# A quarter of a weight conversion moved to GpSimd, an earlier first score, and matmuls padded to one tiling

## The chip, the cores and the metric

The kernel runs on one core of a Trainium2 chip. The metric is the device time of that core in microseconds (us), the median of several executions. A core has five engines that each work through their own list of instructions in order and meet only at semaphores: TensorE (PE, its weight loads shown as PEld), VectorE (DVE), ScalarE (ACT), GpSimd (POOL) and SyncE (SP), which here only issues transfers.

## The reference, cut to what matters

There are 8 batches, 8 heads, 576 tokens and a head size of 64. For each head, attention keeps only the 32 largest scores of a row; the heads are put side by side to a row of 512 channels, and an FNet block with a two-layer channel network follows.

```python
scores = scale * np.matmul(q, k.transpose(0, 1, 3, 2))
kth = np.partition(scores, -32, axis=-1)[..., -32:-31]
scores = np.where(scores >= kth, scores, -1e9)
attn = softmax(scores)                     # exp(scores - max) / (sum + 1e-9)
x = heads_side_by_side(attn @ v)           # (8, 576, 512)
u = x + np.real(fft(fft(x, axis=1), axis=2))
un = (u - mean(u)) / np.sqrt(var(u) + 1e-6)
out = u + np.maximum(un @ w_ch1, 0.0) @ w_ch2   # 512 -> 2048 -> 512
```

The arrays q, k and v are float32; the two weight matrices come as float64[...], so they are converted in the kernel.

## The kernel before, in words

**Items and steps.** Two heads form a pair, so a batch has 4 pairs and the whole input 32. The 576 queries of a head are cut into four blocks of 128 and a tail block of 64 (two times 32 rows, one from each half of the sequence). The tail blocks of both heads of a pair share one tile. A pair therefore has 9 items (`IN_PAIR`), a batch 36 (`PER_BATCH`) and the whole input 288. One main loop over `i` makes one step for each item, and each step puts, by hand, some work on every engine: the scores of item `i + 3` (`scores`), the top-32 search of item `i` and the first half of that of `i + 1` (`top_ops`), the mask (`mask`), the exponential (`expo`), the transposes of the probabilities (`transposes`), and now and then the product with v (`attend`). Work that is due at a given step is stored by `at(step, where, fn)` and is put out when the loop reaches that step and place.

**The top-32 search** is on VectorE: per item four `max` (L350) and three `match_replace` (L352) over 576 scores. Two values per row then go to GpSimd, which forms the bounds `nt` (L359); ScalarE makes from them a penalty (`Relu`, L366); GpSimd subtracts it from the scores (L367); ScalarE takes the exponential (L373); TensorE transposes the result (L394, L405). So each item goes VectorE, GpSimd, ScalarE, GpSimd, ScalarE, TensorE, and GpSimd stands in this chain twice.

**The weight conversion** is in the first batch only. There are 32 chunks of 128x512 numbers, one started in nearly every step (`start_of`). A chunk n with start s0 is loaded as pairs of 32-bit words into one of five slots (`space`). At step s0 + 1 ScalarE scales the high words into a PSUM tile (`scale_high`, L169) and makes two other words ready (`rest`, L185 and L188); VectorE shifts the scaled word left by 3 bits into the weight tile (`shift`, L176); GpSimd adds the low bits and multiplies by the sign (`join`, L195 and L196). When the join is done, the slot is free and chunk n + 5 is loaded. For columns of the first layer, GpSimd also subtracts a mean later (`centre`, L912): eight such instructions fall in the first batch.

**The Fourier part of a batch** begins when its attention is done. VectorE or GpSimd folds the channels (`fold_ops`, `fold_tails`), TensorE multiplies by tables (`dft_tokens`, L594), once for even and once for odd frequencies, so two passes per batch and 16 in all. In a pass, the stationary operand has 128 rows for the two full token blocks (`fg`, `zw`) and 64 for the tail tokens (`ft`). After `dft_channels` the two-layer network (`hidden` L737 and `back` L761) is cut into units that are put between the attention work of the next batch, as a rule of the loop decides (`level`, `some`).

**Tail scores.** The keys of the tail tokens are multiplied in a matmul of their own (`scores` with `part == 1`, L299), with a block-diagonal key tile `kt` of 128x128. For the 128-row items, the stationary operand is 128 queries; for the tail item it is 64. The trace writes the shape of the array that an instruction uses as rows times columns of the stationary operand, such as 128\*64.

**The start.** All of q of pair 0 is loaded and transposed before k; k goes through a tile of its own. The tail scores of item 0 use the same two PSUM tiles as the full scores and are copied by ScalarE.

Of the kernel before, what the change touches and what calls it, by code (L numbers as in the profile page):

```python
# [18 lines left out]
P = 128  # L19
# [45 lines left out]
def kernel(  # L65
# [57 lines left out]
    nat_t = const.tile([P, NC, 2, D], F32, name="nat", tag="nat")  # L123

    kt_t = const.tile([P, P], F32, name="kt", tag="kt")
    v_t = [const.tile([P, NC, 2, D], F32, name=f"v{i}", tag=f"v{i}") for i in range(2)]


# [19 lines left out]
    def weight_steps(chunks, space, wc, slots):  # L148

        scaled = {}  # L150

        def words(n):
            o = 2 * wc * (n % slots)
            raw = space[:, o:o + 2 * wc]
            return raw, raw[:, 0:2 * wc:2], raw[:, 1:2 * wc:2]

        def load(n):
            if n < len(chunks):
                dst, src = chunks[n]
                if moe_w_ch1.dtype == F32:  # L160
                    nc.sync.dma_start(out=dst, in_=src)
                else:
                    nc.sync.dma_start(out=words(n)[0].bitcast(I32), in_=src.bitcast(I32))

        def scale_high(n):
            if moe_w_ch1.dtype == F32:
                return
            scaled[n] = ps_m.tile([P, wc], F32, name=f"wh_{n}", tag="mm")
            nc.scalar.activation(  # L169
                out=scaled[n], in_=words(n)[2], func=AF.Copy, scale=2.0 ** -112  # L170
            )

        def shift(n):
            if moe_w_ch1.dtype == F32:
                return
            nc.vector.tensor_scalar(  # L176
                out=chunks[n][0].bitcast(I32), in0=scaled.pop(n).bitcast(I32),
                scalar1=3, scalar2=None, op0=ALU.logical_shift_left,
            )

        def rest(n):
            if moe_w_ch1.dtype == F32:
                return
            _, low, high = words(n)
            nc.scalar.activation(  # L185
                out=low.bitcast(I32), in_=low.bitcast(U32), func=AF.Copy, scale=2.0 ** -29
            )
            nc.scalar.activation(out=high, in_=high.bitcast(I32), func=AF.Sign)  # L188

        def join(n):  # L190
            if moe_w_ch1.dtype == F32:
                return
            dst, (_, low, high) = chunks[n][0], words(n)
            bits = dst.bitcast(I32)
            nc.gpsimd.tensor_tensor(out=bits, in0=bits, in1=low.bitcast(I32), op=ALU.add)  # L195
            nc.gpsimd.tensor_tensor(out=dst, in0=dst, in1=high, op=ALU.mult)  # L196

        return load, scale_high, shift, rest, join


    nat, qT_of, kT_of, v_of, PT, Ssb, Wk, Wp, M8, Nt = ({} for _ in range(10))
# [3 lines left out]

    def load_full(dst, src, pair, queue=None):
        b, hp = divmod(pair, NPB)
        for e in range(2):  # L210
            s2 = src[b, 2 * hp + e].rearrange("(h r) d -> h r d", h=2)
            for h in range(2):
                (queue or nc.sync).dma_start(
                    out=dst[:, 2 * h:2 * h + 2, e, :],
                    in_=s2[h, 0:2 * P, :].rearrange("(t p) d -> p t d", p=P),
                )

    def load_tails(dst, src, pair, row0=(0, 0)):
        b, hp = divmod(pair, NPB)
        for e in range(2):  # L220
            s2 = src[b, 2 * hp + e].rearrange("(h r) d -> h r d", h=2)
            for h in range(2):
                r0 = row0[e] + TH * h
                nc.sync.dma_start(out=dst[r0:r0 + TH, NF, e, :], in_=s2[h, 2 * P:HS, :])

    def load_nat(n, pair, dst=None, queue=None):
        if pair < NPAIR:
            nat[n, pair] = nat_t if dst is None else dst
            src = q if n == "q" else k
            load_full(nat[n, pair], src, pair, queue)  # L230
            load_tails(nat[n, pair], src, pair)

    def load_v(pair):
# [2 lines left out]
            load_full(v_of[pair], v, pair)  # L236
            load_tails(v_of[pair], v, pair, (0, TAIL))

    def prep(n, pair):

        if pair >= NPAIR:
            return 0.0
        src = nat.pop((n, pair))
        t_sb = attp.tile([P, S if n == "q" else NF * P], F32, name=f"{n}T_{pair}", tag=f"{n}T")
        for c0, c1 in ((0, NF), (NF, NC)):
            tp = ps_t.tile([P, 4, P], F32, name=f"tp{n}_{pair}_{c0}", tag="tp")
            for c in range(c0, c1):
                nc.tensor.transpose(  # L248
                    tp[:, c - c0, :], src[:, c, :, :].rearrange("p h d -> p (h d)"), ident
                )  # L250
            if c0 == 0:
                dst, got = t_sb[:, 0:NF * P], tp.rearrange("p a c -> p (a c)")
            else:
                dst, got = t_sb[:, NF * P:], tp[:, 0, 0:TAIL]
            if n == "q":
                nc.scalar.mul(out=dst, in_=got, mul=scale)
            elif c0 == 0:
                nc.scalar.copy(out=dst, in_=got)
            else:
                for hd in (slice(0, D), slice(D, P)):  # L260
                    nc.scalar.copy(out=kt_t[hd, hd], in_=got[hd])
        (qT_of if n == "q" else kT_of)[pair] = t_sb
        return 0.7


# [8 lines left out]
    def scores(i, part):  # L274
# [20 lines left out]
                (Ssb[i + 1], slice(0, P), slice(TAIL, S), slice(0, TAIL)),  # L295
            ]
        if part == 1:
            sp = ps_s.tile([P, NF * P], F32, name=f"sp_{i}_t", tag="sp")
            nc.tensor.matmul(  # L299
                sp[0:rows, 0:P], lhsT=qT[:, q_cols], rhs=kt_t, start=True, stop=True  # L300
            )
            for h, (s_t, r, _, tails) in enumerate(to):
                nc.scalar.copy(out=s_t[r, tails], in_=sp[0:rows, TAIL * h:TAIL * (h + 1)])  # L303
            return 0.3
        if e is None and i >= PER_BATCH:

# [201 lines left out]
        return ap.rearrange("p (m two) -> p two m", two=2)  # L508

    Q1, Q2, Q3 = DM // 4, DM // 2, 3 * DM // 4  # L510
    ROWS3 = (P, P, TAIL)
    folded, ft_of, y_of, yt_of, us_of, rs_of, unT_of = ({} for _ in range(7))

    def fold_channels(eng, z, f, n):

# [18 lines left out]

    def fold_tails(b, eng):


        z = batp.tile([P, DM], F32, name=f"zt_{b}", tag="fold_s")[0:TAIL]
        ft_of[b] = batp.tile([P, DM + 1], F32, name=f"ft_{b}", tag="fold_t")
        f = ft_of[b][0:TAIL]  # L540
        fold_halves(eng, x_of[b][0:TAIL, 4, :], z)
        for n in range(2):
            fold_channels(eng, z, f[:, 0:DM], n)
        eng.tensor_copy(out=f[:, DM:DM + 1], in_=z[:, Q1:Q1 + 1])
# [34 lines left out]
    def dft_tokens(b, par):  # L579
# [1 line left out]
        while any(u[2] == "hidden" for u in queue):  # L581
            one_unit()
        _, zw, fg = folded[b, par]
        tails = ft_of[b]
        if b not in y_of:
            y_of[b] = batp.tile([P, 4, S], F32, name=f"y_{b}", tag="y")
        y = y_of[b]
# [4 lines left out]
        def mm(g2, gg, st, lhsT, rows, table, start=False):  # L592

            nc.tensor.matmul(  # L594
                yps[g2][0:rows, gg, :],
                lhsT=lhsT[0:ROWS3[st]],
                rhs=fs[0:ROWS3[st], table, par, st, :],
                start=start,
                stop=st == 2,
                skip_group_check=True,  # L600
            )

        for g2 in range(2):
            for gg in range(2):
                g = 2 * g2 + gg
                for st in range(2):
                    mm(
                        g2, gg, st, fg[:, st, P * g:P * (g + 1)], P, gg,  # L610
                        start=gg == 0 and st == 0,
                    )
        for st in range(2):
            mm(0, 1, st, zw[:, st, Q1:Q1 + 1], 1, 0)
        mm(0, 1, 2, tails[:, DM:DM + 1], 1, 0)
        for g2 in range(2):
            for gg in range(2):
                g = 2 * g2 + gg
                mm(g2, gg, 2, tails[:, P * g:P * (g + 1)], P, gg)

        mir, back = (
            (slice(HS + 2, S, 2), slice(KQ - 2, 0, -1)) if par == 0
# [218 lines left out]
    nc.vector.memset(cc[:, 0:1], -1.0)  # L841

    warm = small.tile([P, 1], F32, name="warm", tag="rd", bufs=6)
    nc.scalar.activation(out=warm, in_=cc[:, 0:1], func=AF.Exp)
    nc.vector.memset(cc[:, 1:2], FAR)
    for t in mv + den_t:
        nc.vector.memset(t, 1.0)

    kn0 = batp.tile([P, NC, 2, D], F32, name="kn0", tag="y")
    for t in v_t:  # L850
        nc.gpsimd.memset(t[TAIL:P, NF, 0, :], 0.0)
        nc.gpsimd.memset(t[0:TAIL, NF, 1, :], 0.0)
    for t in (nat_t, kn0):
        nc.gpsimd.memset(t[TAIL:P, NF, :, :], 0.0)
    nc.gpsimd.memset(kt_t, 0.0)

    nc.scalar.dma_start(out=ident, in_=id_d.ap())
    load_nat("q", 0)
    load_nat("k", 0, kn0, nc.scalar)
    prep("q", 0)  # L860
    prep("k", 0)


# [10 lines left out]
    wcs = weight_chunks(w1, moe_w_ch1, NDT, WC) + weight_chunks(w2, moe_w_ch2, NIT, WC)  # L874
    n1 = NDT * DF // WC
    AHEAD = 5
    load, scale_high, shift, rest, join = weight_steps(wcs, sp1, WC, AHEAD)
    for n in range(3):
        load(n)
    load_v(0)  # L880
    load_nat("q", 1)
    nc.sync.dma_start(out=fs, in_=fs_d.ap())
    nc.sync.dma_start(out=fd, in_=fd_d.ap())
    nc.sync.dma_start(out=sg, in_=sg_d.ap())
# [1 line left out]
        load(n)  # L886
    start_of = [0] + [34 * n // len(wcs) for n in range(1, len(wcs))]
    for n, s0 in enumerate(start_of):
        at(s0 + 1, "convert", lambda n=n: scale_high(n))
        at(s0 + 1, "convert", lambda n=n: rest(n))  # L890
        at(s0 + 1, "dve", lambda n=n: shift(n))
        at(s0 + 1, "pool", lambda n=n: join(n))
        at(s0 + 1, "load", lambda n=n: load(n + AHEAD))

# [129 lines left out]
            got += one_unit()  # L1024
        return got

    for j in (0, 2):
        for c in range(2):
            scores(j, c)
    for op in top_ops(0, (0, 1)):  # L1030
        op()
    i, carry = 0, 0.0
# [144 lines left out]
```

## Time and profile before

| what | value |
|---|---|
| time, median of 3 | 1957.48 us (1957.12 to 1959.05) |
| span of the profiled execution | 1955.2 us |
| TensorE matmul busy | 1842.4 us, 94% |
| VectorE busy | 1576.6 us, 81% |
| ScalarE busy | 1202.9 us, 62% |
| GpSimd busy | 773.3 us, 40% |

The shares are means over two stages with different limits. In the first batch, up to about 260 us, TensorE is busy some two thirds of the time and VectorE nearly always. From then to about 1720 us TensorE is nearly always busy, with the network of the batch before between the attention work. The rest is the last batch's Fourier part and network on TensorE alone. A duration of an instruction is the time on its engine; the idle time that stands before it carries the name of what ended it.

### The profile page before, as it was taken

Reading aid. Unit: us, or ns where it says so; the run is one execution under the profiler, and the core shown is the slowest. Engines: PE = TensorE matmul, PEld = TensorE weight load, DVE = VectorE, ACT = ScalarE, POOL = GpSimd, SP = SyncE. Lnnn points to the kernel's source line nnn. Section 1 sums busy time; section 2 is a strip of 40 time slices with the busy share of each in tenths; the row PEclk is TensorE's granted clock in tenths of the full one; section 3 lists DMA queues with packets and bytes.
Section 4 is the critical chain, followed back from the end, with each engine's and each line's share of the span. In section 5 each row is a group of like instructions: output and inputs, shape, how many; then the busy total and the mean of one; then the engine's idle time right before and its main releaser. Section 6 shows DMA issues by size and latency. Waiting matters only on the chain.

```text
span 1955.2 us, 27234 instructions
## 1 busy us (share of the span) xinstructions
PE 1842.4 (94%) x8626; PEld 1117.9 (57%) x8626; DVE 1576.6 (81%) x3240; ACT 1202.9 (62%) x3063; POOL 773.3 (40%) x1056
## 2 busy tenths in 40 slices
PE   6566699999999999999999999999999999998999
PEld 3344465464655656556664756556564756566655
DVE  7999989998999989888888879988888879843000
ACT  6878657776766767666666657666666657541100
POOL 4768642326523444235523444235522444232000
PEclk8787799999999999999999999999999999999999
DMA  5333000101001010010100110010101100000000
GB/s 153 110 94 105 19 13 19 33 19 29 19 19 33 19 25 18 13 33 19 28 20 20 27 24 18 13 33 19 24 18 25 27 24 19 1 14 1 11 14 11
DMA packets 133583, 57.80 MB, mean 30 GB/s; under 512 B 124352, under 2 KB 124480, under 8 KB 133440
## 3 DMA queue, kind: packets, MB, share of 16 engines
q1 hardware_dynamic: 132208, 55.73, 10.8%
q8 instruction: 69, 1.13, 0.2%
q14 instruction: 74, 0.61, 0.1%
q10 hardware_dynamic: 1232, 0.33, 0.1%
HBM read 46.57 MB, written 9.44 MB: 29 GB/s over the span
## 4 chain that ended last, share of the span: by engine, by line
PE 80%; DVE 8%; POOL 6%; issue 3%; ACT 2%; DMA 0%; POOLq 0%; SPq 0%; DVEq 0%; ACTq 0%
PE hp L737 24%; PE cp L761 22%; PE o L431 7%; PE tpP L394 6%; PE sp L329 5%; DVE m L350 4%; PE yp L594 3%; DVE wk L352 3%; PE cp L797 3%; PE mp L651 2%; POOL wk L367 2%; PE sp_t L299 2%; POOL w L196 1%; POOL w L195 1%; PE tpk L248 1%
## 5 line engine op out<-in xcount | busy, mean ns | idle before, releaser
L367 POOL TENSOR_TENSOR wk<-S,wk 128x576 f32<-128x576 f32 x288 | 407.0, 1413 | 917.5 <-ACT wk L366 863.4
L350 DVE MAX8 m<-wk 128x8 f32<-128x576 f32 x864 | 623.2, 749 | 5.5
L737 PE MATMUL hp<-unT,w 128*128 128x256 f32 (+1 forms) x2048 | 539.5, 410 | 2.5 <-ACT unT L718 2.1
L761 PE MATMUL cp<-w,hT 128*128 128x512 f32 x1024 | 478.5, 599 | 0.0
L737 PEld LDWEIGHTS hp<-unT,w 128*128 128x128 f32 x2048 | 373.9, 191 | 126.2 <-issue 32.3
L352 DVE MATCH_REPLACE8 wk<-m,wk 128x576 f32<-128x576 f32 x576 | 427.5, 742 | 0.0
L761 PEld LDWEIGHTS cp<-w,hT 128*128 128x128 f32 x1024 | 179.5, 190 | 182.2 <-issue 181.4
L373 ACT ACTIVATE wk<-wk,nt 128x576 f32<-128x576 f32 x288 | 224.8, 781 | 53.5 <-POOL wk L367 52.2
L394 PE MATMUL tpP<-ident,wk 128*128 128x128 f32 x1152 | 185.8, 286 | 68.2 <-ACT wk L373 45.7
L397 ACT COPY PT<-tpP 128x512 f32<-128x512 f32 (+1 forms) x320 | 171.0, 545 | 124.1 <-PE tpP L394 121.4
L366 ACT ACTIVATE wk<-S,nt 128x576 f32<-128x576 f32 x288 | 226.9, 788 | 27.4 <-POOL nt L359 26.2
L394 PEld LDWEIGHTS tpP<-ident,wk 128*128 128x128 f32 x1152 | 140.0, 145 | 167.0 <-ACT wk L373 63.1
L350 DVE MAX8 m<-S 128x8 f32<-128x576 f32 x288 | 213.9, 743 | 23.0 <-ACT S L303 22.6
L741 ACT ACTIVATE hT<-hp 128x320 f32<-128x320 f32 (+1 forms) x256 | 104.7, 409 | 197.4 <-PE hp L737 195.1
L352 DVE MATCH_REPLACE8 wk<-m,S 128x576 f32<-128x576 f32 x288 | 213.6, 742 | 0.0
L431 PE MATMUL o<-PT,v 128*64 128x256 f32 (+3 forms) x1440 | 193.9, 413 | 1.9 <-ACT PT L397 1.4
L332 ACT COPY S<-sp 128x512 f32<-128x512 f32 (+1 forms) x264 | 142.0, 589 | 66.2 <-PE sp L329 65.9
L329 PE MATMUL sp<-kT,qT 64*128 64x512 f32 (+1 forms) x528 | 160.1, 668 | 4.0 <-ACT means L916 3.1
L431 PEld LDWEIGHTS o<-PT,v 128*64 128x64 f32 x1440 | 110.8, 152 | 74.7 <-issue 15.9
L775 DVE SCALAR_TENSOR_TENSOR x<-cp,gi,x 128x512 f32<-128x512 f32 x11 | 8.2, 746 | 128.3 <-PE cp L761 128.3
L299 PEld LDWEIGHTS sp_t<-kt,qT 128*128 128x128 f32 (+1 forms) x322 | 51.4, 187 | 58.6 <-issue 22.2
L329 PEld LDWEIGHTS sp<-kT,qT 64*128 64x128 f32 (+1 forms) x528 | 42.5, 191 | 61.1 <-issue 44.6
(124 smaller groups left out, 1798.2 us busy)
## 6 DMA issues: line engine op xcount, KB each, us to landing
space<-in_moe_w_ch_dram SPq DMA_DIRECT2D x32, 512.0 KB, 3.7
nat<-in_q_dram SPq DMA_DIRECT2D x128, 64.0 KB, 2.1
v<-in_v_dram SPq DMA_DIRECT2D x128, 64.0 KB, 2.2
out_dram<-x SPq DMA_DIRECT2D x32, 256.0 KB, 2.1
nat<-in_k_dram SPq DMA_DIRECT2D x124, 64.0 KB, 2.2
nat<-in_q_dram SPq DMA_DIRECT2D x128, 8.0 KB, 1.8
v<-in_v_dram SPq DMA_DIRECT2D x128, 8.0 KB, 1.8
nat<-in_k_dram SPq DMA_DIRECT2D x124, 8.0 KB, 1.7
```

The costliest lines, as they stand in the source:

```text
L329: nc.tensor.matmul(sp[r], lhsT=qT[hd, q_cols], rhs=kT[hd, :], start=True, stop=True)
L332: nc.scalar.copy(out=s_t[r, keys], in_=sp[r])
L350: ops.append(lambda src=src, m8=m8: nc.vector.max(out=m8, in_=src))
L352: ops.append(lambda src=src, m8=m8: nc.vector.match_replace(w, m8, src, NEG))
L366: nc.scalar.activation(out=w, in_=Ssb[i], func=AF.Relu, scale=-FAR, bias=Nt[i][:, 1:2])
L367: nc.gpsimd.tensor_tensor(out=w, in0=Ssb.pop(i), in1=w, op=ALU.subtract)
L373: nc.scalar.activation(out=w, in_=w, func=AF.Exp, bias=Nt.pop(i)[:, 0:1], accum_out=den_t[pair % 3][:, c:c + 1],)
L394: nc.tensor.transpose(tp[:, c, :], p_sb[:, k0 + P * c:k0 + P * (c + 1)], ident)
L397: nc.scalar.copy(out=pt[:, NF * he:NF * (he + 1), col:col + w], in_=tp[:, :, o:o + w])
L431: nc.tensor.matmul(o[D * e:D * (e + 1), c0:c1], lhsT=vv[:, c, e, :], rhs=pt[:, 2 * NF if c == NF else NF * e + c, c0:c1], start=(c == 0), ...
L737: nc.tensor.matmul(hp[:, 0:w], lhsT=w1[:, dt, P * it:P * (it + 1)], rhs=unT[:, dt, 0:w], start=(dt == 0), stop=(dt == NDT - 1),)
L761: nc.tensor.matmul(cp, lhsT=hT[:, it, P * n:P * (n + 1)], rhs=w2[:, it, :], start=(it == 0), stop=(it == NIT - 1),)
```

## The change

It has three parts.

1. Every fourth chunk (n = 3, 7, ... 31, eight of 32) is not shifted on VectorE. ScalarE writes the scaled word straight into the weight tile, three steps earlier (s0 - 2), and GpSimd doubles it three times, as a wrapping integer sum of the tile with itself, at steps s0 - 2, s0 - 1 and s0. It is meant to take work off VectorE in the first batch.
2. The first scores wait only for half of q: two q loads come first, k follows on two queues, the second half of q is transposed after the scores of items 0 and 1. The tail scores of item 0 get a PSUM tile from another pool and are copied by VectorE. Loads and fills at the start are reordered; the load of the second pair's q moves behind the weight chunks 0 to 4.
3. The matmuls of the tails use all 128 rows and columns of the array: the tail item's tail scores take 128 queries of which the last 64 count, and the folded tails live in one tile `ftail` whose other 64 rows are zero for good. In `dft_tokens` the tail matmul now follows its group's two full blocks, and the single-column matmuls stand together at the end.

```diff
+        def double(n):
+            if moe_w_ch1.dtype == F32:
+                return
+            bits = chunks[n][0].bitcast(I32)
+            nc.gpsimd.tensor_tensor(out=bits, in0=bits, in1=bits, op=ALU.add)
...
     for n, s0 in enumerate(start_of):
-        at(s0 + 1, "convert", lambda n=n: scale_high(n))
+        own = n % 4 == 3
+        at(s0 - 2 if own else s0 + 1, "convert", lambda n=n, own=own: scale_high(n, own))
         at(s0 + 1, "convert", lambda n=n: rest(n))
-        at(s0 + 1, "dve", lambda n=n: shift(n))
+        if own:
+            for r in range(3):
+                at(s0 - 2 + r, "pool", lambda n=n: double(n))
+        else:
+            at(s0 + 1, "dve", lambda n=n: shift(n))
         at(s0 + 1, "pool", lambda n=n: join(n))
...
-            sp = ps_s.tile([P, NF * P], F32, name=f"sp_{i}_t", tag="sp")
+            pool, tag = (ps_s, "sp") if i else (ps_m, "mm")
+            copy = nc.scalar.copy if i else nc.vector.tensor_copy
+            sp = pool.tile([P, NF * P], F32, name=f"sp_{i}_t", tag=tag)
+            q_end = P * t + rows
             nc.tensor.matmul(
-                sp[0:rows, 0:P], lhsT=qT[:, q_cols], rhs=kt_t, start=True, stop=True
+                sp[:, 0:P], lhsT=qT[:, q_end - P:q_end], rhs=kt_t, start=True, stop=True
             )
...
-                lhsT=lhsT[0:ROWS3[st]],
-                rhs=fs[0:ROWS3[st], table, par, st, :],
+                lhsT=lhsT,
+                rhs=fs[:, table, par, st, :],
...
+                for st in range(3):
+                    f = fg[:, st] if st < 2 else ftail
+                    mm(g2, gg, st, f[:, P * g:P * (g + 1)], P, gg, start=gg == 0 and st == 0)
+        for st in range(3):
+            mm(0, 1, st, zw[:, st, Q1:Q1 + 1] if st < 2 else ftail[:, DM:DM + 1], 1, 0)
...
-    load_nat("q", 0)
-    load_nat("k", 0, kn0, nc.scalar)
-    prep("q", 0)
+    nat["q", 0], nat["k", 0] = nat_t, kn0
+    nc.scalar.dma_start(out=ident, in_=id_d.ap())
+    for e in range(2):
+        load_half(nat_t, q, 0, e, 0)
+    for e in range(2):
+        load_half(kn0, k, 0, e, 1, nc.scalar)
+        load_half(kn0, k, 0, e, 0)
...
+    prep("q", 0, ((0, 2),))
     prep("k", 0)
...
-    for j in (0, 2):
-        for c in range(2):
-            scores(j, c)
+    for c in range(2):
+        scores(0, c)
+    prep("q", 0, ((2, NF), (NF, NC)))
+    load_nat("q", 1)
+    for c in range(2):
+        scores(2, c)
```

## The prediction, made before the run

> **What bounds the kernel now.** I read the page's table of slices first, to see that there are two stages, then the chain of waits of the first one, then the timeline of GpSimd in it, and last the timeline of TensorE in the second.
>
> ```profile
> PE   6566699999999999999999999999999999998999
> DVE  7999989998999989888888879988888879843000
> POOL 4768642326523444235523444235522444232000
> ```
>
> A slice is 49 us. In slices 1 to 5 (the first batch) VectorE is full and TensorE is not; afterwards TensorE is. It looks as if the first batch were VectorE's alone. The chain of waits, followed back from the end and read between 107 and 118 us, says otherwise:
>
> ```profile
> 107.27 1.42 POOL wk L367
> 108.69 1.25 POOL w L195
> 110.01 1.29 POOL w L196
> 111.30 0.15 POOL nt L359
> 111.45 0.85 issue
> 112.34 1.41 POOL wk L367
> ```
>
> GpSimd's mask, its two joins, its bounds, then 0.85 us in which it only waits for ScalarE's penalty: that is a whole step, without a gap. GpSimd's timeline has the same step elsewhere (start, duration, then in brackets the idle time before):
>
> ```profile
> 61.03 1.42 POOL L367 TENSOR_TENSOR wk<-S,wk 128x576 f32<-128x576 f32 x1 [0.89 <-ACT wk L366]
> 62.40 1.29 POOL L195 TENSOR_TENSOR w<-w,space 128x512 int32<-128x512 int32 x1
> 63.78 1.30 POOL L196 TENSOR_TENSOR w<-w,space 128x512 f32<-128x512 f32 x1
> 65.03 0.19 POOL L359 TENSOR_TENSOR nt<-m,cc 128x2 f32<-128x2 f32 x1
> 66.11 1.42 POOL L367 TENSOR_TENSOR wk<-S,wk 128x576 f32<-128x576 f32 x1 [0.89 <-ACT wk L366]
> ```
>
> From mask to mask 5.08 us, against 5.56 us that VectorE needs for an item and its shift (L350 at 27.44, 33.00, 38.56). The waits between 20 and 240 us (total, times, longest):
>
> ```profile
> POOL wk L367 <- ACT wk L366: 55.6, 37, 4.8
> POOL nt L359 <- DVE m L350: 6.4, 5, 2.6
> ```
>
> In 220 us GpSimd waited for VectorE 6.4 us in all. The rest of its idle time, 55.6 us, is the wait for the penalty: 37 times the unavoidable 0.89 us is 33 us, and 22.7 us more where ScalarE was late. So GpSimd, 66% busy between 40 and 140 us, has hardly any time that it could give.
>
> In the second stage the windows say that TensorE is busy 1192.81 of 1200 us between 500 and 1700 us. There the timeline shows what a change of array shape costs:
>
> ```profile
> 648.22 1.89 PE L737 MATMUL hp<-unT,w 128*128 128x256 f32 x8
> 649.95 0.60 PE L394 MATMUL tpP<-ident,wk 128*128 128x128 f32 x4
> 650.48 0.66 PE L314 MATMUL sp<-kT,qT 64*64 64x256 f32 x8
> 651.08 1.99 PE L737 MATMUL hp<-unT,w 128*128 128x256 f32 x8
> 653.00 0.43 PE L299 MATMUL sp_t<-kt,qT 128*64 128x128 f32 x2
> 653.36 1.99 PE L737 MATMUL hp<-unT,w 128*128 128x256 f32 x8
> 655.19 0.60 PE L394 MATMUL tpP<-ident,wk 128*128 128x128 f32 x4
> ```
>
> Read starts, not durations, which overlap. Eight network matmuls with the same shape on both sides take 1.73 us (648.22 to 649.95), after another shape 1.83, with another on both sides 1.92.
>
> **What the Trainium skill says.** "TensorEngine Tiling (Array Packing)", Key Properties: a change of tiling mode drains TensorE; the trace agrees, at about 0.1 us for each change. "GPSIMD Engine Reference", Engine selection: a sum of two int32 tiles into an int32 tile is exact and wraps, so a doubling is an ordinary two-input sum; this trace prices the same form at 1.29 us (L195). "Perfetto Trace Analysis", Tensor Engine Instruction: ScalarE, VectorE and GpSimd are strict queues; the trace agrees, since no join starts in the 0.89 us before a mask.
>
> **Part 1, the doublings.** Removed: 8 shifts of 0.68 us from VectorE, some 5.3 us, in a stage where it is nearly full. Added: 24 doublings on GpSimd. Each takes 1.25 us from start to start (L196 to the next instruction, 63.78 to 65.03), 30.0 us in all. They stand behind the join of their step, so in the queue the next item's bounds and mask are behind each, and behind these ScalarE's exponential and TensorE's transposes. A step with a doubling is 5.08 + 1.25 = 6.33 us on GpSimd, and VectorE needs 4.9 or 5.56. GpSimd becomes the bound.
>
> What can hide a doubling is a wait that follows it in the next step, listed from the timeline by item: late penalties beyond 0.89 us at items 6 (1.90), 10 (0.56), 14 (0.86), 15 (1.79), 19 (3.9), 20 (1.69), 22 to 32 (small ones), 33 (1.0), and VectorE's late results at 4 (0.45), 12 (0.79), 13 and 14 (0.4 each). With each counted to at most 1.25 us and only behind a doubling, this is 10.9 us. So 30.0 - 10.9 = 19.1 us are added.
>
> Moving eight scalings (0.62 us, L169) three steps ahead puts them between a penalty and an exponential where ScalarE is already the late one (items 1, 5, 9, 18, 26, partly 13): 5 x 0.62 + 0.3 = 3.4 us. Their loads: chunk 7 is issued when the join of chunk 2 ends, lands 3.7 us later (median), and is wanted about 3.95 us later; no wait, but barely. Chunk 3 is wanted in the first step, right behind 1.4 MB of tables in the queue: up to 2 us late, I take 1. Together 23.5 us on GpSimd's way from item 1 to item 35, which took 199.0 us (24.83 to 223.81).
>
> Bounds: without any late penalty this way is 34 steps x 5.08, less 2 x 2.6 for the steps without a join, plus 8 x 1.23 (L912), which gives 177.4, and with 30.0 it is 207.4, or 8.4 more than now. With all late penalties kept and nothing hidden but VectorE's waits, some 26 more.
>
> **Part 2, the start.** TensorE's first scores began at 8.94 us, VectorE at 12.83. With k and half of q first, k's tails leave the queue near 3.7 instead of 6.67, and scores begin near 6.85: 2.1 us. The tail scores no longer wait for ScalarE to free a tile, and VectorE copies them itself (two copies of 0.2): some 0.8 more. 2.9 us, all of it on the path, since GpSimd's first bounds wait for VectorE. At the end of the batch 1.0 us comes back too: the normalised tile was ready at 233.6 and VectorE, still in its search, took it at 234.64; now VectorE waits there. So the fold of batch 0 (235.17 us) comes 23.5 - 2.9 - 1.0 = 19.6 us later. Everything behind it is in order on TensorE and has no slack, so this goes to the end.
>
> **Part 3, the padding.** A tail item in batches 1 to 7: now 651.08 to 655.19, 4.11 us for network, tail scores, network. With one shape only the first change is left: 1.83 + 0.22 (two matmuls at 128x128, 645.73 to 645.95) + 1.73 = 3.78. Gain 0.33 x 28 = 9.2 us. A token pass: at 723.61 the 16 records of the full blocks take 2.07 us, the single columns 0.59, the tails 1.52. At the rate inside one shape (256 columns take 1.73 / 8 = 0.216, so 145 columns about 0.123) the 30 records are 3.7 us, and two changes of 0.1 stay: 3.9 instead of 4.2. Gain 0.3 x 16 = 4.8. Sum 14.0; I count 12, since in batch 1 TensorE is only 191.85 of 200 us busy. The added rows cost nothing: with 145 columns a record of 128 rows lasts 304 ns in the mean, one of 64 rows 293 (L594).
>
> **Sum.** 1957.5 + 19.6 - 12 = 1965.1, rounded to 1965 us.
>
> **The rivals.** (a) GpSimd's idle time hides the doublings and VectorE sets the first batch: it is 98.94 of 100 us busy from 40 to 140 us, which speaks for it. Then 5.3 + 2.9 + 12 are gained: 1937. Against it speak the 0.89 us waits, which no queue in order can fill. (b) ScalarE's lateness vanishes once GpSimd is slower, the lower bound: 8.4 - 2.9 - 1.0 = 4.5 more, less 12: 1950. For it: ScalarE already waits for GpSimd 11.6 us. (c) GpSimd as forecast, but the time freed on TensorE turns into waits, since VectorE is at 1061.63 of 1200 us and its steps may set the pace: only the four passes of batches 0 and 7, 1.2 us, stay, 1957.5 + 19.6 - 1.2 = 1976.
>
> **How the numbers follow.** Forecast 0.58, which with its terms uncertain by some 5 us spreads over 1955 to 1972; (a) 0.13, (b) 0.12, (c) 0.17. Faster by over 0.2% (under 1953.6): (a) and most of (b), 0.23. Same: the rest of (b) and the lower edge of the forecast, 0.13. Slower (over 1961.4): 0.64. With a tenth left out at each side the range is 1948 to 1976.
>
> **What would show it.** Right: VectorE starts near 9.9 us; bounds L383 to bounds some 6.3 us apart in steps with a doubling; the bounds of item 35 near 240 us; VectorE with gaps before 240 us; the fold some 20 us later; L323 all 128\*128 and its neighbour 0.1 us shorter. Wrong: VectorE still without gaps and the fold before 235 us (a), or second stages of equal length (c).

## The result, and the profile after

The changed kernel takes 1969.89 us (median of 4, 1968.41 to 1970.73) against 1957.3 us (1956.74 to 1959.05) of the kernel before on the same chip: a ratio of 1.0062, 95% interval 1.0045 to 1.0079. It is slower by 12.6 us. The forecast was 1965 us.

The page's table of slices for the changed kernel, to be read against the one of before:

```profile
span 1968.1 us, 27252 instructions
...
PE   4565689999899999999999999999999999998999
...
DVE  6888889999899999988889888888889888853000
...
POOL 3768833325633364225532444225533454232000
```

A slice is again 49 us, and the first one is slice 0. In slices 1 to 4 VectorE (DVE) has fallen from 9 to 8, and in slice 4 GpSimd (POOL) has risen from 6 to 8: VectorE no longer fills the first batch. The chain of waits of the changed kernel, in a step with a doubling:

```profile
88.01 0.99 POOL w L188
89.00 0.15 POOL nt L383
89.15 0.85 issue
...
90.04 1.42 POOL wk L391
91.46 1.24 POOL w L204
...
92.78 1.29 POOL w L205
94.07 1.00 POOL w L188
95.07 0.15 POOL nt L383
95.22 0.85 issue
```

From bounds (L383) to bounds is 6.07 us. That is the step of before plus one doubling (L188); in this chain it costs 1.00 us from start to start. The 0.85 us of waiting for ScalarE's penalty stands in the step as before, behind the doubling and not under it.

The waits of the changed kernel between 20 and 255 us (total, times, longest), and the windows (busy time of each engine in each stretch):

```profile
POOL wk L391 <- ACT wk L390: 59.5, 36, 10.0
...
ACT wk L390 <- POOL nt L383: 22.3, 19, 2.8
...
DVE m L374 <- ACT S L327: 16.5, 14, 2.4
```

```profile
40.00:140.00 100.00, 57.10 (x297) 37.97 (x295) 89.95 (x181) 78.81 (x183) 76.14 (x75) 0.73 0.33 99
...
500.00:1700.00 1200.00, 1186.37 (x5791) 730.99 (x5790) 1065.55 (x2210) 802.25 (x2051) 491.20 (x703) 1.00 0.09 22
```

The first of these rows in the kernel before:

```profile
40.00:140.00 100.00, 64.99 (x328) 41.46 (x327) 98.94 (x204) 80.96 (x190) 65.74 (x65) 0.76 0.36 102
```

After the length of the stretch a row has the busy time of TensorE, its weight loads, VectorE, ScalarE and GpSimd, then TensorE's granted clock, the share of the DMA engines and GB/s. GpSimd waits for VectorE no more: the line of before that named it is gone. VectorE falls from 98.94 to 89.95 us in the first row; it now waits for others. In the second row TensorE is nearly full, as before (1186.37 of 1200 us, before 1192.81). One wait has a new size: GpSimd's longest wait for a penalty is 10.0 us, against 4.8 before. It is the first one. The timelines of GpSimd, ScalarE and TensorE at the start of the changed kernel:

```profile
27.33 1.42 POOL L391 TENSOR_TENSOR wk<-S,wk 128x576 f32<-128x576 f32 x1 [10.01 <-ACT wk L390]
28.70 0.19 POOL L383 TENSOR_TENSOR nt<-m,cc 128x2 f32<-128x2 f32 x1
33.76 1.42 POOL L391 TENSOR_TENSOR wk<-S,wk 128x576 f32<-128x576 f32 x1 [4.86 <-ACT wk L390]
```

```profile
25.88 0.71 ACT L275 ACTIVATE qT<-tpq 128x512 f32<-128x512 f32 x2 [11.02 <-PE tpq L267]
26.48 0.78 ACT L390 ACTIVATE wk<-S,nt 128x576 f32<-128x576 f32 x1
```

```profile
24.75 1.30 PE L267 MATMUL tpq<-ident,nat 128*128 128x128 f32 x5 [10.31 <-DMA nat<-in_q_dram]
```

The same places in the kernel before, in order of time:

```profile
17.20 1.20 PE L248 MATMUL tpq<-ident,nat 128*128 128x128 f32 x4 [0.69 <-DMA nat<-in_q_dram]
18.43 0.60 ACT L256 ACTIVATE qT<-tpq 128x512 f32<-128x512 f32 x1 [1.50 <-PE tpq L248]
19.97 0.77 ACT L366 ACTIVATE wk<-S,nt 128x576 f32<-128x576 f32 x1
20.82 1.42 POOL L367 TENSOR_TENSOR wk<-S,wk 128x576 f32<-128x576 f32 x1 [0.88 <-ACT wk L366]
```

Read the three of the changed kernel from below. TensorE transposes q of the second pair at 24.75 us, when its load lands. ScalarE scales the transposed tile (L275) at 25.88 and had been idle for 11.02 us in front of it. The penalty of item 0 (L390) is the next instruction behind that in ScalarE's queue, so it starts at 26.48 instead of 19.97; GpSimd has waited for it since its bounds. The load was issued at 17.70 us, behind weight chunks 0 to 4, v and the tables; before, at 13.93, ahead of the tables.

Where the 12.6 us come from, with the marks in the two traces (us from the start of the span):

| mark | before | after | after minus before |
|---|---|---|---|
| mask of item 1 | 26.79 | 33.76 | +7.0 |
| mask of item 35 | 226.95 | 249.06 | +22.1 |
| fold of batch 0 on VectorE | 235.17 | 257.18 | +22.0 |
| token pass of batch 2 | 689.35 | 710.67 | +21.3 |
| token pass of batch 7 | 1777.59 | 1791.08 | +13.5 |
| end of the span | 1955.2 | 1968.1 | +12.9 |

The first batch loses 22.0 us, the later ones win 9.1 back.

### The profile page after: what moved, and what is told of

The parts are those of the page before. It is cut to its first block, busy times and chain, and to the rows that moved or that the text cites. A ratio compares the mean times of both kernels' runs of the same rounds, so it can differ in the third digit from the quotient of the medians.

```text
span 1968.1 us, 27252 instructions
## 1 busy us (share of the span) xinstructions
PE 1832.2 (93%) x8626; PEld 1125.0 (57%) x8626; DVE 1575.0 (80%) x3237; ACT 1207.3 (61%) x3062; POOL 796.6 (40%) x1078
## 4 chain that ended last, share of the span: by engine, by line
PE 77%; POOL 11%; DVE 5%; issue 4%; ACT 2%; DMA 1%; SPq 0%; POOLq 0%; ACTq 0%; DVEq 0%
PE hp L749 24%; PE cp L773 21%; PE o L455 7%; PE tpP L418 5%; PE sp L353 5%; POOL wk L391 3%; PE yp L614 3%; PE cp L809 3%; PE mp L663 2%; POOL w L205 2%; POOL w L204 2%; DVE m L374 2%; PE sp_t L323 2%; DVE wk L376 2%; POOL w L188 1%
## 5 line engine op out<-in xcount | busy, mean ns | idle before, releaser
L773 PE MATMUL cp<-w,hT 128*128 128x512 f32 x1024 | 477.2, 597 | 0.0
L773 PEld LDWEIGHTS cp<-w,hT 128*128 128x128 f32 x1024 | 179.4, 190 | 180.5 <-issue 179.9
L390 ACT ACTIVATE wk<-S,nt 128x576 f32<-128x576 f32 x288 | 227.7, 790 | 38.5 <-POOL nt L383 37.0
L323 PEld LDWEIGHTS sp_t<-kt,qT 128*128 128x128 f32 x322 | 57.0, 198 | 51.3 <-issue 19.6
```

The lines of the kernel that those rows point to most:

```text
L390: nc.scalar.activation(out=w, in_=Ssb[i], func=AF.Relu, scale=-FAR, bias=Nt[i][:, 1:2])
L773: nc.tensor.matmul(cp, lhsT=hT[:, it, P * n:P * (n + 1)], rhs=w2[:, it, :], start=(it == 0), stop=(it == NIT - 1),)
```

## The experiments

Ratios are to the kernel before, with 95% intervals; "fold" is the start of batch 0's fold on VectorE (235.17 us before, 257.18 after).

**e1: the kernel before with the doublings alone** (`double` and the scaling in place as in the change).

```diff
+        own = n % 4 == 3
+        at(s0 - 2 if own else s0 + 1, "convert", lambda n=n, own=own: scale_high(n, own))
+        if own:
+            for r in range(3):
+                at(s0 - 2 + r, "pool", lambda n=n: double(n))
+        else:
+            at(s0 + 1, "dve", lambda n=n: shift(n))
```

> The kernel before, with the doublings alone (eight chunks scaled three steps early and doubled three times on GpSimd; start and padding as before). Theory A, GpSimd's queue is the bound of the first batch and the doublings lengthen it: 24 doublings at 1.0 us from start to start, less about 9 us of waits that hide some of them: 1957.4 + 15 = 1972 us (1968 to 1976), bounds of item 35 near 239 us, gaps on VectorE. Theory B, VectorE is the bound and the changed kernel's loss is all in its start: eight shifts of 0.68 us fewer, 1952 to 1958 us.

Measured: 1977.92 us (1977.02 to 1981.87), 1.0113 (1.0097 to 1.0128), fold at 256.40. The doublings alone cost 21 us: theory A, and past its upper end. The mask of item 35 comes 216.5 us after that of item 1, as against 200.2 before: +16.3. Another 4.6 us are lost ahead of item 1's mask (31.42 as against 26.79), on ScalarE's timeline in e1:

```profile
26.38 0.66 ACT L169 ACTIVATE w<-space 128x512 f32<-128x512 f32 x1 [3.56 <-DMA space<-in_moe_w_ch_dram]
```

The early scaling of chunk 3 waits 3.56 us for its load, and the exponential of an item and the next penalty stand behind it. The trace is of the longest of the four runs (1981.87 us). It loses a further 3.7 us behind the fold: from the second token pass of batch 1 to the first of batch 2 it takes 202.8 us at a granted clock of 0.98 for TensorE, before 199.1 at 1.00.

**e2: the kernel before with both paddings alone.**

```diff
-                sp[0:rows, 0:P], lhsT=qT[:, q_cols], rhs=kt_t, start=True, stop=True
+                sp[:, 0:P], lhsT=qT[:, q_end - P:q_end], rhs=kt_t, start=True, stop=True
...
-                lhsT=lhsT[0:ROWS3[st]],
-                rhs=fs[0:ROWS3[st], table, par, st, :],
+                lhsT=lhsT,
+                rhs=fs[:, table, par, st, :],
```

> The kernel before, with the padded matmuls alone. Theory A, the second stage is TensorE's and shape changes cost it 0.1 to 0.2 us each: 1957.4 - 9 = 1948 us (1946 to 1951), as much as the changed kernel made good between its first fold and its end. Theory B, that gain came from the later start of the second stage, with VectorE further ahead, and not from the padding: 1955 to 1958 us.

Measured: 1946.6 us (1945.89 to 1947.18), 0.9948 (0.9931 to 0.9964), fold at 234.82. As A expected, the padding brings 10.4 us, all of it after the fold, which has hardly moved.

**e7: the tail scores' padding alone** (the first two lines of the diff of e2, in the kernel before).

> The kernel before, with the tail items' tail scores padded and nothing else. Theory A, 0.33 us for each of 28 tail items, realised where TensorE is full: 1957 - 6 = 1951 us (1949 to 1953), about 60% of what both paddings bring. Theory B, the gain is in the token passes: 1955 to 1957 us.

Measured: 1949.3 us (1949.2 to 1949.38), 0.996 (0.9945 to 0.9975): 7.7 of the 10.4 us. The token passes are left with 2.7.

**e3: the changed kernel, with the second pair's q loaded sooner.**

```diff
     for n in range(3):
         load(n)
+    for c in range(2):
+        scores(0, c)
+    prep("q", 0, ((2, NF), (NF, NC)))
+    load_nat("q", 1)
+    for n in range(3, AHEAD):
+        load(n)
     load_v(0)
```

(The same lines are taken out where they stood: the scores, transposes and load of q at the first scores, the load of chunks 3 and 4 behind the tables.)

> The changed kernel, with the first scores, the second half of q and the load of the second pair's q put ahead of weight chunks 3 and 4, of v and of the tables. Theory A, the start lost time because that load came late and ScalarE's first penalty stands behind the second pair's transposed q: the first penalty near 17.5 us instead of 26.48, and 1969.9 - 9 = 1961 us (1959 to 1964). Theory B, a late start is made good by the waits of the first batch: 1967 to 1970 us.

Measured: 1960.35 us (1959.67 to 1962.1, 12 runs), 1.0018 (1.001 to 1.0027), fold at 248.65. As A expected, the place of one load in a queue is worth some 9.5 us. (The edit also puts chunks 3 and 4 ahead of v and the tables, but in the changed kernel no engine waited for any of these in the first batch.) GpSimd's timeline of e3 shows the start as it had been forecast:

```profile
17.80 1.42 POOL L391 TENSOR_TENSOR wk<-S,wk 128x576 f32<-128x576 f32 x1 [0.89 <-ACT wk L390]
```

The first mask is at 17.80 us and its wait is the common 0.89; after the change alone it was at 27.33, before the change at 20.82.

**e4: the changed kernel without doublings.**

```diff
-        own = n % 4 == 3
+        own = False
```

> The changed kernel with no chunk doubled: all 32 are scaled in their own step and shifted by VectorE. Theory A, doublings cost some 15 us: 1969.9 - 15 = 1955 us (1950 to 1957); the first penalty stays near 26.5 us. Theory B, doublings are hidden and only the start costs: 1967 to 1972 us.

Measured: 1951.14 us (1950.27 to 1951.67), 0.9972 (0.996 to 0.9984), fold at 237.66. Within A's range: with the late start kept, the doublings cost 18.7 us.

**e5: both edits, of e3 and of e4.**

> The changed kernel without doublings and with the second pair's q loaded early: padding and early start alone. Theory A, with VectorE the bound of the first batch its early start reaches the end: fold of batch 0 near 232 us, 1946.6 - 3 = 1943.5 us (1942 to 1946). Theory B, GpSimd and ScalarE have so little spare time that an early start is eaten up by item 35: the same as the padding alone, 1945.5 to 1947.5 us.

Measured: 1943.56 us (1942.04 to 1944.01), 0.9929 (0.9915 to 0.9944), fold at 231.01. This is the shortest time of the study, 13.5 us under the kernel before. It is e2 with the new start in its better order, and 3.0 us shorter than e2 (its fold comes 3.8 us earlier): that is what the new start brings when no late load undoes it.

**e6: e3 with half of the doublings** (`own = n % 8 == 7`).

> As the kernel with the early load and without doublings, but with every eighth chunk (four of 32) doubled on GpSimd. Theory A, GpSimd has 5.56 - 5.08 = 0.5 us of slack in a step, 16 us in the batch, of which subtractions take 10: twelve doublings of 1.0 us cost more than the four shifts of 0.68 us bring: 2 to 7 us slower than without doublings. Theory B, some share pays, only a quarter is too much: 1 to 3 us faster than without.

Measured: 1954.78 us (1951.44 to 1957.3, 20 runs), 0.9986 (0.998 to 0.9993), fold at 240.39. It is 11 us slower than e5, where 2 to 7 were expected. So half of the doublings are not mostly hidden: 12 at the 0.7 us that each of the 24 costs in e3 (16.8 / 24) are 8.4 us. ScalarE's timeline of e6 names another part:

```profile
41.95 0.67 ACT L171 ACTIVATE w<-space 128x512 f32<-128x512 f32 x1 [0.54 <-DMA space<-in_moe_w_ch_dram]
...
91.28 0.68 ACT L171 ACTIVATE w<-space 128x512 f32<-128x512 f32 x1 [1.17 <-DMA space<-in_moe_w_ch_dram]
```

A chunk's load begins with the end of the join of the chunk five places before it. A scaling three steps earlier leaves it three steps less, and with fewer doublings the steps are shorter: in e3 no scaling waited for a load, here two did, 1.7 us together. By the traces 9.4 us stand ahead of the fold; 1.7 us are lost behind it, from batch 1's second token pass to batch 2's first, where the granted clock was 0.99 (199.5 us) and in e5 1.00 (197.8 us).

**e8: e1 with chunk 3 shifted on VectorE as before** (`own = n % 4 == 3 and n > 3`).

> The kernel before with seven chunks doubled, all but chunk 3. Theory A, of the 21 us that the eight cost, 4 to 5 are chunk 3's scaling, which in the first step waits 3.56 us for its load with ScalarE's queue behind it, and 2 to 3 its own three doublings: 1970 to 1972 us, mask of item 1 near 27 us instead of 31.42. Theory B, the early wait is made good later: 1974 to 1976 us, the share of three doublings in 24 alone.

Measured: 1974.32 us, but between 1970.75 and 1976.51, 1.0086 (1.0071 to 1.0101). The median speaks for B, while the trace has the mask of item 1 at 26.95 (31.42 in e1) and the fold at 250.94 (256.40), as A said; here a later load was awaited, for 0.60 us. With this spread the medians don't decide. The two traces do, as far as one run of each can: both are of the longest run of their kernel and both take 202.8 us for the stretch of e1 where the clock was 0.98, and e8's ends 5.4 us earlier (1974.7 and 1980.0 us), 4.5 us of it gained at item 1's mask already. In these two runs chunk 3's wait is not made good later, as A said.

**e9: e3, with the doublings put into GpSimd's wait**, between the bounds of an item and its mask.

```diff
-                at(s0 - 2 + r, "pool", lambda n=n: double(n))
+                at(s0 - 2 + r, "gap", lambda n=n: double(n))
...
         bounds(i)
+        run(i, "gap")
         if i < PER_BATCH:
             mask(i)
```

> The kernel e3 (changed kernel with the second pair's q early) with one further edit: the doublings stand in GpSimd's queue between the bounds of an item and its mask, where GpSimd has 0.89 us of wait for ScalarE's penalty in every step, and no longer behind the joins. Theory A (the cost of a doubling is its place in the queue: behind the join it stands ahead of the next bounds and so delays everybody; between bounds and mask ScalarE works on the penalty meanwhile): a step with a doubling goes from 6.07 us on GpSimd to about 5.2 (5.07 + 1.0 - 0.89), which is under VectorE's 5.56 for an item with its shift, so VectorE is the bound again. The fold of batch 0 then lies at 227 to 233 us (231.0 without any doubling, in e5; up to 5.3 us of shifts saved, up to 3 given back by early scalings), the time at 1939 to 1946 us; VectorE busy 95 us or more of 40 to 140. Theory B (the place doesn't matter: what counts is GpSimd's sum of work, or the early scalings on ScalarE, which make the penalty as late as before): steps stay at about 6 us, the idle time ahead of the mask stays 0.5 us or more, the fold stays near 248 and the time 1956 to 1962.

Measured: 1950.29 us (1948.5 to 1950.99), 0.9962 (0.9948 to 0.9976), fold at 240.0. The same instructions in the same step cost 10 us less than in e3. GpSimd's timeline of e9:

```profile
60.20 0.19 POOL L383 TENSOR_TENSOR nt<-m,cc 128x2 f32<-128x2 f32 x1
60.34 1.04 POOL L188 TENSOR_TENSOR w<-w 128x512 int32<-128x512 int32 x1
61.34 1.42 POOL L391 TENSOR_TENSOR wk<-S,wk 128x576 f32<-128x576 f32 x1
62.71 1.29 POOL L204 TENSOR_TENSOR w<-w,space 128x512 int32<-128x512 int32 x1
64.08 1.29 POOL L205 TENSOR_TENSOR w<-w,space 128x512 f32<-128x512 f32 x1
65.33 0.19 POOL L383 TENSOR_TENSOR nt<-m,cc 128x2 f32<-128x2 f32 x1
66.41 1.42 POOL L391 TENSOR_TENSOR wk<-S,wk 128x576 f32<-128x576 f32 x1 [0.89 <-ACT wk L390]
```

The mask at 61.34 has no wait ahead of it, and the one at 66.41, in a step without a doubling, has the full 0.89 us. From bounds to bounds a step with a doubling takes 5.13 us (60.20 to 65.33), where it took 6.07. So far A is right. The time missed A's 1939 to 1946, since the early scalings now waited for their loads, as in ScalarE's timeline of e9:

```profile
43.92 0.66 ACT L171 ACTIVATE w<-space 128x512 f32<-128x512 f32 x1 [2.37 <-DMA space<-in_moe_w_ch_dram]
```

**e10: e9 with scaling and doublings one step later** (`s0 - 1` for `s0 - 2` in both places; the last doubling then stands in the step of the join, ahead of it).

> The kernel e9 with the whole of a doubled chunk's preparation one step later: the scaling at s0 - 1, the doublings at s0 - 1, s0 and s0 + 1, each between bounds and mask, the last of them in the step of the join and ahead of it. e9 showed the doublings in GpSimd's wait (steps with one take 5.06 to 5.15 us), but early scalings waited for their chunk's load, 5.4 us in four waits, and items 5, 9 and 13 came 9.46, 7.43 and 6.85 us after the item before. Theory A (these waits, on ScalarE ahead of the exponential and the next penalty, are what keeps e9 from its 1939 to 1946 us): with some 5 us more for each load the waits of the scalings for a load fall to under 1 us in all, item 5 comes 7 us or less after item 4, the fold of batch 0 lies at 229 to 235 us (240.0 in e9) and the time at 1940 to 1946 us. Theory B (it is the scaling itself, put between a penalty and an exponential where ScalarE is the late one, or the load is late whatever the step): the fold stays at 237 to 241 and the time at 1947 to 1952.

Measured: 1945.16 us (1944.26 to 1946.9), 0.9941 (0.9925 to 0.9958), fold at 235.1. The waits of scalings for loads are gone from the list of waits, and item 5's mask comes 6.42 us after item 4's, where it was 9.46. So by the medians 24 doublings can be had for 1.6 us more than none (e5), by the fold for 4.1 us (235.1 and 231.0), but they bring nothing either: VectorE, freed of 5.3 us of shifts, is busy 95.61 of 100 us between 40 and 140, where e5 has 98.97.

## Why the prediction was right, and where it was not

The direction and the range held. The sum came out 5 us short, with one term of the wrong sign and another too large: the start was forecast at -2.9 us and brought +6.5 (-3.0 and +9.5), the doublings came 5.7 us lower than forecast. That the sum was so near is in part luck, since these two errors have opposite signs. The runs make a ladder from the kernel before to the changed one, each rung the difference of two medians:

| rung | from, to | measured us | forecast us |
|---|---|---|---|
| the padding | before 1957.0, e2 1946.6 | -10.4 | -12 |
| the new start, q of pair 1 in time | e2, e5 1943.6 | -3.0 | -2.9 |
| the doublings | e5, e3 1960.4 | +16.8 | +22.5 (23.5 - 1.0) |
| q of pair 1 behind chunks and tables | e3, after 1969.9 | +9.5 | not seen |

A rung is not exact to the tenth. From the second token pass of batch 1 to the first of batch 2 the traces of e3, e5, e9 and e10 take 197.8 us at a granted clock of 1.00 for TensorE; those of the changed kernel, e2, e4 and e6 take 199.4 to 199.5 us at 0.99, with the same matmuls (16 of them, L663, take 4.88 us in the changed kernel at 519.26 and 3.62 in e3 at 510.57). The fold lies ahead of this stretch. By the fold the four rungs are -0.3, -3.8, +17.6 and +8.5 us: the doublings and the load keep their size, and the new start's agreement with its forecast to 0.1 us is chance.

**"Part 1, the doublings": mechanism right, one size wrong.** GpSimd bounds the first batch and VectorE has gaps, as the step said. It took a doubling as long as the join, 1.25 us from start to start. The changed kernel's timeline shows 24 doublings, each with one tile as both inputs, in groups by operation:

```profile
L205 POOL TENSOR_TENSOR w<-w,space 128x512 f32<-128x512 f32 x32 | 41.3, 1292 | 2.5
L204 POOL TENSOR_TENSOR w<-w,space 128x512 int32<-128x512 int32 x32 | 41.3, 1290 | 0.0
L188 POOL TENSOR_TENSOR w<-w 128x512 int32<-128x512 int32 x24 | 25.0, 1041 | 0.0
```

The mean (after the bar, in ns) is 1041, where the joins take 1290. So 24 x 1.0 = 24 us were added, not 30. From the mask of item 1 to that of item 35 the way grew by 15.1 us, not 23.5: GpSimd's busy time there by 23.5 us (144.6 to 168.2), while its other time fell by 8.4 (55.5 to 47.1). The step forecast 10.9 us hidden, less 4.4 for early scalings and chunk 3's load, a net of 6.5. (The waits that it lists behind a doubling sum to 10.5; the 0.4 at item 13 stands behind none.) Of the 8.4 us, 4.7 are waits of the bounds, which are gone (3.86 for VectorE and 0.87 for TensorE before, in this stretch), and 3.6 are penalties that come less late (48.2 and 44.6 us of waiting ahead of the masks). Of the difference to the forecast, 6 us are the duration and 2 us the net. In the changed kernel, with its late start, chunk 3's scaling waited for no load; in e1, with the old start, it waited 3.56 us, against the 1 us that I took.

That the 0.89 us waits could not be filled was argued against rival (a). It holds for the place that the change chose, behind the joins; e9 shows that a doubling between bounds and mask fills them. "Perfetto Trace Analysis", Tensor Engine Instruction, in the Trainium skill calls GpSimd a strict queue, and e9 agrees with it: what decided was the order in which the instructions stand.

**"Part 2, the start": the step that failed.** It counted 2.9 us gained, "all of it on the path, since GpSimd's first bounds wait for VectorE". VectorE did gain: its first `max` began at 10.21 us instead of 12.83, behind two copies that began at 9.87, near the 9.9 that was forecast. But the path went elsewhere. I followed the first scores and did not follow the load of the second pair's q, which the change moved back; it is put at nothing, without a reason. The late load delays TensorE's transposes, these delay ScalarE's scaling of q, and that delays the first penalty, which is next in ScalarE's queue. Instead of 2.9 us earlier, item 1 was 7.0 us later. That the load's place is the cause is shown by e3: with the load ahead of the tables the first mask comes at 17.80 us instead of 27.33, and the run is 9.5 us shorter. "DMA: Bandwidth & Descriptors", Queues, rings and completion order, says that on each DMA engine a ring's descriptors are consumed in order; the trace fits that. The issues of the changed kernel between 10 and 20 us (count, KB each, median us to landing):

```profile
space<-in_moe_w_ch_dram SPq DMA_DIRECT2D x2, 512.0 KB, 6.5
fs<-c_fs SPq DMA_DIRECT2D x1, 870.0 KB, 4.6
fd<-c_fd SPq DMA_DIRECT2D x1, 512.0 KB, 5.5
nat<-in_q_dram SPq DMA_DIRECT2D x4, 64.0 KB, 6.1
```

The same four loads between 10 and 20 us in the kernel before:

```profile
nat<-in_q_dram SPq DMA_DIRECT2D x4, 64.0 KB, 2.2
```

In the changed kernel they stand behind 2.4 MB (2 x 512 + 870 + 512 KB) and take 6.1 us to land; before, ahead of the tables, they took 2.2. So the load is issued 3.8 us later than before (17.70 against 13.93), and lands later by some 4 us more.

The 1.0 us that should have come back at the end of the batch did not: from the mask of item 35 to the fold it is 8.1 us after and 8.2 before. VectorE was late with its search there as it had been.

**"Part 3, the padding": mechanism right, its sum too large.** In the changed kernel's timeline of TensorE, a tail item:

```profile
1045.92 1.98 PE L773 MATMUL cp<-w,hT 128*128 128x512 f32 x4
1047.74 0.38 PE L323 MATMUL sp_t<-kt,qT 128*128 128x128 f32 x2
1047.96 1.88 PE L773 MATMUL cp<-w,hT 128*128 128x512 f32 x4
1049.68 0.60 PE L418 MATMUL tpP<-ident,wk 128*128 128x128 f32 x4
```

From 1045.92 to 1049.68 it is 3.76 us, where 3.78 was forecast and 4.11 measured before (with L737 in place of L773, which takes as long). The tail scores take 0.22 us with both neighbours in the same shape. A token pass takes 4.01 and 3.90 us (1582.73 to 1586.74, 1621.54 to 1625.44), as against 4.28 and 4.18 (1567.69 to 1571.97, 1607.10 to 1611.28): 0.27 to 0.28 saved where 0.3 was forecast. Of the full sum of 14.0 us I counted 12, and 10.4 came (e2): 7.7 for the tail scores instead of 9.2 (e7), and 2.7 for the passes instead of 4.8. In e7's trace 23 of the 28 tail items save 0.29 to 0.34 us each and five save 0.13 or nothing, 7.5 us in all; why these five don't was not followed. In the changed kernel the later passes gain some 1.55 us a batch (19.75, 18.2, 16.55, 15.0, 13.5 us behind the kernel before in batches 3 to 7). From the fold to batch 1's first token pass 0.7 us are gained (22.0 to 21.3 us behind), and from there to batch 2's first nothing (21.3 at both). The reserve of 2 us had as its reason that TensorE is not full in batch 1. For the stretch without a gain the traces show another one: between batch 1's second pass and batch 2's first the granted clock was 0.99 in the changed kernel and in e2 (199.5 us) and 1.00 in the kernel before (199.1 us); e5, with the same padding at 1.00, takes 197.8 us and has its gain there too.

**The rivals.** (a), VectorE as the bound at 1937 us, and (b), late penalties that vanish at 1950, were refuted by the fold, which came 22.0 us later. (c), TensorE's freed time turning into waits, was refuted by the second stage: fold to end of span 1710.9 us, as against 1720.0. Of the other marks, the bounds of item 35 came at 245.82 us where near 240 was forecast, and from bounds to bounds it was 6.07 us, not 6.3.

**What stays open.** Why a doubling is shorter than a sum of two tiles was not tried. What bounds e10, where neither VectorE nor GpSimd is full, is not settled either.

## What to carry to other kernels

Before an engine's work is moved to another one with idle time, look at where in that engine's queue the idle time stands and put the work there: here a doubling of 1.0 us cost the run 0.7 us behind a join (e5 to e3), and between bounds and mask, with the loads in time, less than 0.2 us (e5 to e10). When a change brings some loads forward, follow those that it moves back to their consumers, and see which instruction stands in the queue behind each consumer. Work that is done some steps earlier needs its inputs that much earlier; the number of load slots has to be counted again.

## What the runs showed of the hardware

A sum on GpSimd with the same tile as both inputs takes 1.04 us for 128x512 int32, against 1.29 us with two tiles, in all 24 and 32 cases (1.033 to 1.053 and 1.279 to 1.299). A tail matmul of a token pass with 128 rows, half of them zero, costs no more than one with 64: two of them take 0.24 us from start to start (1583.34 to 1583.58), and ten of before took 1.52 us, changes of shape included (1609.76 to 1611.28). TensorE's granted clock can differ from kernel to kernel in one and the same stretch, here between the token passes of batches 1 and 2: with all matmuls padded the stretch takes 197.8 us at 1.00 and 199.5 us at 0.99, with none padded 199.1 us at 1.00 and 202.8 us at 0.98 (one trace of each kernel).
